# The opening of a fused attention and SoLU kernel: order of a table load, of loads, of masks and of a conversion

## The chip, the core and the metric

The kernel runs on one core of a Trainium2 chip. The time is the device time of one execution in microseconds (us); before the change it is 384.42 us, the median of four runs (383.80 to 385.46). The engines are named as in the profile: PE (TensorE matmuls; PEld its weight loads), DVE (VectorE), ACT (ScalarE), POOL (GpSimd), SP (SyncE, which here only issues DMAs).

## The reference

Gated linear attention over 4 batches x 8 heads, 768 tokens, head width 48, followed by a SoLU block with a normalisation on the same 3072 tokens (8 x 48 = 384 columns):

```python
for t in range(S):
    state = alpha[:, :, t, :, None] * state + einsum('bhd,bhe->bhde', k[:, :, t], v[:, :, t])
    y[:, :, t] = einsum('bhd,bhde->bhe', q[:, :, t], state)
...
h = x @ w_in                                  # 384 -> 1024
e = exp(h - max(h)); sm = e / (sum(e) + 1e-9)
solu = h * sm
ln = (solu - mean(solu)) / sqrt(var(solu) + 1e-6) * g_ln
out = ln @ w_out                              # 1024 -> 384
```

The inputs q, k, v and alpha are float32; the two weight matrices arrive as float64.

## The kernel before

The tokens are worked in G = 6 chunks of 128. In a chunk the recurrence is written as matrices: running products of alpha are applied to the keys and the queries, scores of 128 x 128 tokens are taken for each batch and head, masked to the lower triangle (by one mask, since the scores stand transposed), and multiplied with v; what earlier chunks contribute comes through a state. The four batches lie on four groups of 32 partitions. A head's first 32 columns fill such a group; the last 16 columns of two heads share one. So there are NB = 12 blocks: 8 of first columns and 4 of last columns, in three tiles of four blocks (tile 2 holds the last columns).

The whole order is written out by hand: each engine runs its instructions in the order of the program, and nothing reorders them. The change touches only the opening, that is the loads and chunk 0. There the steps are these, with their lines:

- DMA issues. SP issues alpha, k, q (two DMAs each, `load_first`, L153), v as one DMA of 768 KB into slot 0 of a buffer `room` (`load_v_first`, L188), then the first two weight requests (`fetch`, L559): three DMAs of 512 KB for the pieces 0 and 1 of w_in into slots 3 and 4, and three for the pieces 2 and 3 into slots 1 and 2. ScalarE issues four small ones (identity, mask, parity, gains; L640 to L644).
- POOL clears buffers (L647 to L653), then moves v from the slot into its padded place vn, the even and the odd heads apart (two copies, L190).
- PE warms up with 18 products of a constant tile (`warm`, L442; each call counts two records in the profile) and then turns alpha, k and q by products with the identity (`turned`, L171). ScalarE brings the last columns together first (`ends_of`, L162; its first instruction is preceded by the load of its function tables) and copies the turned alpha to SBUF (L671).
- DVE takes the running products (`scan_back` and `scan_on`, both L219), multiplies the turned keys (L679) and the turned queries (L689) by them: first tile 2 of the queries (`qe`), then tiles 0 and 1. ScalarE splits `qe` by parity (`apart`, L244) and checks alpha's range (`alpha_over`, L211).
- PE takes the scores (`scores`, L278) of the heads 0 to 3 into four PSUM banks, one for each batch, and of the heads 4 to 7 into four more. DVE multiplies all eight by the mask into `sT` (`masked`, L289).
- DVE converts piece 0 of w_in from float64 to float32 in five instructions (`bits`, L589, L592, L597, L600, L601). The function can also be called for its first two or its last three alone; so it is already used for later pieces.
- PE multiplies the masked scores with vn (`read_values`, L312): for each batch 16 products, all of a batch's heads; ScalarE copies the result out (L348). Then PE turns the gains (L612) and the keys back (`keys_back`, L297), and ScalarE copies those (L299) and checks the range of the pieces 0 and 1 (`in_range`, L576, L577), while DVE converts piece 1.
- After that the loop over f (from L708) runs the first up-projection (`up_mm`, L386), its exponentials (L400), products (L401) and squares (L402), between the conversions of the other pieces.

Later chunks overlap attention and the SoLU block in the same way. A second function, `general_path`, holds a slower version that runs only if the range checks fail; it is not run here.

Of the kernel before, what the change touches and what calls it, by code (L numbers as in the profile page):

```python
# [9 lines left out]
FP = mybir.dt.float32  # L10
# [4 lines left out]
ALU = mybir.AluOpType  # L15
AX = mybir.AxisListType
P = 128
# [15 lines left out]
def fast_path(ctx, tc, q, k, v, alpha, moe_w_in, moe_w_out, moe_g_ln, out):  # L33
# [12 lines left out]
    nc = tc.nc  # L46
    B, H, S, D = q.shape
# [4 lines left out]
    NP = H // 2  # L52
    NB = H + NP
# [8 lines left out]
    def pool(name, bufs, **kw):  # L62
        return ctx.enter_context(tc.tile_pool(name=name, bufs=bufs, **kw))
# [5 lines left out]
    small = pool("small", 4)  # L69
# [4 lines left out]
    ps_a = pool("ps_a", 1, space=PS)  # L74
# [4 lines left out]
    mask = const.tile([P, P], FP, name="mask")  # L79
# [7 lines left out]
    mhalf = const.tile([P, 1], FP, name="mhalf")  # L87
# [13 lines left out]
    qn = const.tile([P, H, TQ, D], FP, name="qn")  # L101
# [12 lines left out]
    all_of = [slice(0, D), slice(E1, VW)]  # L114
# [17 lines left out]
    sT = const.tile([P, B, H, P], FP, name="sT")  # L132
# [13 lines left out]
    def by_token(x):  # L146

        return x.rearrange("p h u d -> p (h u d)").rearrange("p (b h d) -> p b h d", b=B, h=H)
# [9 lines left out]
    def ends_of(src, tag=None):  # L158

        ends = ring.tile([P, T4], FP, name=tag) if tag else two.tile([P, T4], FP, tag="two", name="ends")  # L160
        ends = ends.rearrange("p (b d) -> p b d", b=B)
        nc.scalar.copy(out=ends.rearrange("p b (h d) -> p b h d", h=H), in_=by_token(src)[:, :, :, E0:D])  # L162
        return ends

    def turned(src, ends, out, blocks=range(NB)):

        x = by_token(src)
        for j in blocks:
            for b in range(B):
                cols = x[:, b, j, 0:E0] if j < H else ends[:, b, E0 * (j - H) : E0 * (j - H) + E0]  # L170
                nc.tensor.matmul(  # L171
                    out[j // NP][32 * b : 32 * b + 32, j % NP], lhsT=cols, rhs=ident, start=True, stop=True,
                    tile_position=(0, 32 * b), skip_group_check=True,
                )
# [8 lines left out]

    def load_v_first(slot):
        x = slots[slot].rearrange("p (n d) -> p n d", d=D)
        y = vn.rearrange("p b h d -> p (b h) d")
        xi, yi = (z.rearrange("p (n i) d -> p i n d", i=2) for z in (x, y))
        nc.sync.dma_start(out=x, in_=v[:, :, 0:P].rearrange("b h p d -> p (b h) d"))  # L188
        for i in range(2):
            nc.gpsimd.tensor_copy(out=yi[:, i, :, all_of[i]], in_=xi[:, i])  # L190


    def firsts(src, dst):
# [90 lines left out]
    masks = {}  # L284

    def masked(half, batches=range(B)):
        a = masks[half]
        for b in batches:
            nc.vector.tensor_tensor(  # L289
                out=sT[:, b, half * NP : half * NP + NP], in0=a[b], in1=mask[:, None, :].to_broadcast([P, NP, P]),  # L290
                op=ALU.mult,
            )
# [25 lines left out]
    def read_begin():  # L318
        reading["y"] = {}
        reading["begun"] = set()  # L320
# [19 lines left out]
    def read_values(g, batches=range(B)):  # L340
        if 0 in batches:
            gr[g]["x"] = pair.tile([P, KC, B, P], FP, name="x")
        for b in batches:
            for n, part in enumerate(parts):
                for a, r, h, e in part:
                    y_mm(b, a, r, 0, vn[:, b, h, e], sT[:, b, h], n == len(parts) - 1)
        for b in batches:
            nc.scalar.copy(out=gr[g]["x"][:, :, b], in_=reading["y"][b])  # L348
# [90 lines left out]
    def warm(n, ps=ps_o, tag="o"):  # L439
        t = ps.tile([P, 512], FP, tag=tag, name="warm")  # L440
        for i in range(n):
            nc.tensor.matmul(t[:, 0:P], lhsT=ones, rhs=ones, start=True, stop=True)  # L442
# [99 lines left out]
    def place(i):  # L542
        kind, f = pieces[i]
        return w_out[:, f : f + 2, 0:DM] if kind else w_in[:, :, f * P : f * P + 2 * P]
# [3 lines left out]
    def fetch(i, slot, n=1):  # L548

        kind, f = pieces[i]  # L550
        w = n * F // (2 if kind else KC)
        raw = room[:, 1536 * slot : 1536 * (slot + n)].bitcast(U32).rearrange("p (c f w) -> p c f w", f=w, w=2)
        if kind:
            parts = [(slice(0, P), c, moe_w_out[(f + c) * P : (f + c + 1) * P, :]) for c in range(2)]
        else:
            parts = [(slice(0, P), c, moe_w_in[c * P : (c + 1) * P, f * P : f * P + w]) for c in range(KC)]
        for rows, c, src in parts:
            if float64:
                nc.sync.dma_start(out=raw[rows, c].rearrange("p f w -> p (f w)"), in_=src.bitcast(U32))  # L559
            else:  # L560
                dst = w_out[rows, f + c, 0:DM] if kind else w_in[rows, c, f * P : f * P + w]
                nc.sync.dma_start(out=dst, in_=src)
        for m in range(n):
            raws[i + m] = raw[:, :, w // n * m : w // n * (m + 1)]
# [14 lines left out]
    def bits(i, part=None):  # L579
        if not float64:  # L580
            return
        lo, hi = raws[i][:, :, :, 0], raws[i][:, :, :, 1]
        if part != 1:
            made[i] = [
                two.tile([P, F], FP, tag="two", name=x).rearrange("p (c f) -> p c f", c=hi.shape[1])
                for x in ("top", "low")
            ]
            top = made[i][0].bitcast(U32)
            nc.vector.tensor_scalar(  # L589
                out=top, in0=hi, scalar1=3, scalar2=0x3FFFFFF8, op0=ALU.logical_shift_left, op1=ALU.bitwise_and  # L590
            )
            nc.vector.scalar_tensor_tensor(  # L592
                out=top, in0=hi, scalar=0xC0000000, in1=top, op0=ALU.bitwise_and, op1=ALU.bitwise_or
            )
        if part != 0:
            top, low = made.pop(i)
            nc.vector.tensor_scalar(  # L597
                out=low.bitcast(U32), in0=top.bitcast(U32), scalar1=0xFF800000, scalar2=None, op0=ALU.bitwise_and
            )
            nc.vector.scalar_tensor_tensor(out=low, in0=lo, scalar=2.0**-52, in1=low, op0=ALU.mult, op1=ALU.mult)  # L600
            nc.vector.tensor_tensor(out=place(i), in0=low, in1=top, op=ALU.add)  # L601
# [49 lines left out]
    nc.gpsimd.memset(hT[:, NB * SW : NB * SW + 2], 1.0)  # L651
    nc.gpsimd.memset(seed, 0.0)
    nc.gpsimd.memset(state, 0.0)  # L653
    load_v_first(0)
    fetch(0, 3, 2)
    fetch(2, 1, 2)
    nc.vector.memset(ones, 1.0)
    nc.vector.memset(small_ones, 1.0 / 32)
# [4 lines left out]
    def three(name, where):  # L663
        return [pool.tile([P, NP, P], FP, tag=tag, name=f"{name}{i}") for i, (pool, tag) in enumerate(where)]


    warm(18)
    t = three("tp_a", [(ps_a, "a0"), (ps_a, "a1"), (ps_a, "a2")])
    turned(an, ends_of(an), t)
    for i in range(3):  # L670
# [2 lines left out]
    t = three("tp_k", [(ps_a, "a3"), (ps_h, "h"), (ps_h, "h")])  # L673
# [5 lines left out]
        nc.vector.tensor_tensor(out=kT[:, part], in0=t[i], in1=hk[:, part], op=ALU.mult)  # L679
    scan_on(0, 0)  # L680
    t = three("tp_q", [(ps_o, "o"), (ps_o, "o"), (ps_a, "a0")])
    turned(qn, ends_of(qn), t)

    warm(2, ps_a, "a1")
    for i in (2, 0, 1):
        if i == 1:
            scan_on(0, i)
# [2 lines left out]
            out=qe if i == 2 else qv[:, part], in0=t[i], in1=aT[:, part, 1:SW], op=ALU.mult  # L690
# [4 lines left out]
    t = [x.tile([P, NP, P], FP, tag=n, name="a_" + n) for x, n in ((ps_h, "h"), (ps_o, "o")) for _ in range(2)]  # L695
    scores(0, 1, t)
    read_begin()
    masked(0)
    masked(1)
    bits(0)  # L700
    read_values(0)
    gains()
    keys_back(0)
# [4 lines left out]
    for f in range(FC):  # L708
        p = 2 + f // 2
# [215 lines left out]
    def compare(out, x, bound, op):  # L925
# [6 lines left out]
        out=chunks[:, :, 2], in0=sums[:, :, 2], scalar=0.25, in1=sums[:, :, 3], op0=ALU.mult, op1=ALU.is_le  # L932
# [6 lines left out]
    else:  # L939
# [9 lines left out]
        out=bad, in0=all_ok[0:1, 0:1], scalar1=float(P * ends[-1]), scalar2=None, op0=ALU.is_lt  # L949
# [415 lines left out]
def kernel(tc, *args):  # L1365

    with ExitStack() as ctx:
        taken = fast_path(ctx, tc, *args)
    with tc.If(taken > 0):
        general_path(tc, *args)  # L1370
# [30 lines left out]
```

## Time and profile before

| What | Value |
|---|---|
| median of four runs | 384.42 us |
| the profiled execution | 385.19 us |
| its span in the profile | 383.4 us |
| granted TensorE clock | 0.998 |
| PE busy (matmuls) | 367.8 us, 96% of the span |
| DVE, ACT, POOL busy | 245.2, 144.4 and 126.0 us |
| HBM read and written | 25.30 and 4.72 MB |

The span is what the engines did; the execution's time is 1.8 us longer. The page cuts the span into 40 slices of 9.6 us and shows how busy each engine was in each, in tenths (9 is 90% or more):

```profile
PE   8879999879899999999999999999999999999995
DVE  0988888996989866893565884665885411444410
ACT  2618775284526244124252224351224131233110
POOL 5020000041045990544521553630562520333210
DMA  9982989303447200961000960001500000000011
```

The opening is the first three digits: PE waits now and then (8, 8, 7), DVE starts in the second slice, and the DMA engines are full until some 27 us. A busy PE is not PE at its peak: its matmuls are pipelined and their ends are modelled.

### The profile page before, as it was taken

What the parts mean: (1) busy time and instruction counts of PE and PEld (TensorE: products, weight loads), DVE (VectorE), ACT (ScalarE), POOL (GpSimd) and SP (SyncE); (2) the same over time, 40 slices, a digit from 0 to 9 for tenths busy, and PEclk for the clock granted to TensorE, in tenths of its full rate; (3) what the DMA queues carried; (4) which work ended last, traced back from release to release, by engine and by line L of the source; (5) the groups of instructions that cost most, each with busy time, mean ns of one, the idle gap of its engine ahead of it and who ended that gap; (6) DMA issues with size and microseconds to landing.
All of it is one profiled execution on the core that took longest, in us unless ns stands there. A gap on an engine that the chain in (4) does not pass through costs nothing.

```text
span 383.4 us, 10525 instructions
## 1 busy us (share of the span) xinstructions
PE 367.8 (96%) x4665; PEld 222.1 (58%) x4665; DVE 245.2 (64%) x381; ACT 144.4 (38%) x258; POOL 126.0 (33%) x132
## 2 busy tenths in 40 slices
PE   8879999879899999999999999999999999999995
PEld 8776345547655656555666555575555665555552
DVE  0988888996989866893565884665885411444410
ACT  2618775284526244124252224351224131233110
POOL 5020000041045990544521553630562520333210
PEclk9999999999999999999999999999999999999999
DMA  9982989303447200961000960001500000000011
GB/s 184 197 297 71 231 261 181 85 21 91 117 111 121 43 4 4 174 151 47 22 3 24 199 148 24 23 10 31 89 0 22 22 24 2 21 21 21 22 45 47
DMA packets 65510, 30.78 MB, mean 80 GB/s; under 512 B 47016, under 2 KB 63664, under 8 KB 65456
## 3 DMA queue, kind: packets, MB, share of 16 engines
q1 hardware_dynamic: 64432, 29.10, 34.2%
q8 instruction: 38, 0.62, 0.7%
q10 hardware_dynamic: 1024, 0.92, 0.7%
q14 instruction: 16, 0.13, 0.1%
HBM read 25.30 MB, written 4.72 MB: 78 GB/s over the span
## 4 chain that ended last, share of the span: by engine, by line
PE 70%; DVE 18%; ACT 6%; issue 3%; DMA 1%; SPq 0%; POOL 0%; DVEq 0%; ACTq 0%
PE o L497 28%; PE h L386 23%; PE y L312 8%; PE a L278 5%; DVE aT L219 3%; DVE hT L219 3%; DVE room L401 2%; PE warm L442 2%; DVE sT L289 1%; ACT sq L576 1%; DVE aT L194 1%; DMA an<-in_alpha_dram 1%; PE kv L361 1%; DVE top L592 1%; ACT sq L577 1%
## 5 line engine op out<-in xcount | busy, mean ns | idle before, releaser
L497 PE MATMUL o<-w_out,room 128*128 128x385 f32 x384 | 133.6, 491 | 2.4 <-DVE o_mean L523 2.4
L386 PE MATMUL h<-x,w_in 128*128 128x512 f32 x288 | 132.1, 598 | 0.4 <-DVE room L401 0.4
L497 PEld LDWEIGHTS o<-w_out,room 128*128 128x128 f32 x384 | 71.3, 190 | 58.5 <-issue 15.9
L386 PEld LDWEIGHTS h<-x,w_in 128*128 128x128 f32 x288 | 53.0, 189 | 59.0 <-issue 48.4
L401 DVE TENSOR_TENSOR room<-h,e 128x512 f32<-128x512 f32 x40 | 27.6, 689 | 82.9 <-ACT e L400 82.7
L400 ACT ACTIVATE e<-h 128x512 f32<-128x512 f32 x40 | 23.9, 597 | 108.6 <-PE h L386 108.6
L527 POOL TENSOR_TENSOR r<-sums,mhalf 128x1 f32<-128x1 f32 x20 | 14.3, 714 | 138.7 <-DVE sums L519 138.7
L417 POOL TENSOR_TENSOR p<-p,e 128x512 f32<-128x512 f32 x30 | 41.8, 1393 | 15.7 <-ACT e L400 15.7
L402 ACT ACTIVATE u<-room 128x512 f32<-128x512 f32 x40 | 25.2, 630 | 35.1 <-DVE room L401 35.1
L289 DVE TENSOR_TENSOR sT<-a,mask 128x512 f32<-128x512 f32 x44 | 27.3, 681 | 9.8 <-PE a L278 9.6
L219 DVE TENSOR_TENSOR_SCAN hT<-aT,unit 128x516 f32<-128x516 f32 x18 | 23.2, 1357 | 8.7 <-ACT aT L671 8.7
L240 POOL TENSOR_TENSOR kT<-kT,hT 128x1024 f32<-128x1024 f32 (+1 forms) x8 | 14.2, 1794 | 43.6 <-DVE kT L194 34.7
L278 PEld LDWEIGHTS a<-qv,kT 32*128 32x128 f32 x704 | 22.3, 186 | 9.2 <-issue 3.5
L278 PE MATMUL a<-qv,kT 32*128 32x128 f32 x704 | 25.5, 279 | 2.0 <-DVE qv L689 0.8
L219 DVE TENSOR_TENSOR_SCAN aT<-aT,seed 128x516 f32<-128x516 f32 x18 | 27.1, 1539 | 0.2
L417 DVE TENSOR_TENSOR p<-p,u 128x512 f32<-128x512 f32 x30 | 23.0, 766 | 6.5 <-ACT u L402 6.5
L312 PE MATMUL y<-sT,vn 128*32 128x128 f32 x768 | 24.0, 274 | 3.0 <-issue 2.1
L312 PEld LDWEIGHTS y<-sT,vn 128*32 128x32 f32 x768 | 21.2, 110 | 5.3 <-issue 3.9
L211 ACT ACTIVATE sq<-an,mone 128x1536 uint8<-128x1536 f32 x12 | 18.9, 1571 | 0.2
L312 PE MATMUL y<-qv,state 32*32 32x128 f32 x960 | 16.8, 277 | 0.1
L529 ACT ACTIVATE o_sb<-o,r 128x384 f32<-128x384 f32 x16 | 9.3, 580 | 18.7 <-POOL r L527 18.7
L312 PEld LDWEIGHTS y<-qv,state 32*32 32x32 f32 x960 | 12.1, 103 | 7.3 <-issue 5.2
(140 smaller groups left out, 368.3 us busy)
## 6 DMA issues: line engine op xcount, KB each, us to landing
an<-in_alpha_dram SPq DMA_DIRECT2D x20, 192.0 KB, 4.0
vn<-in_v_dram SPq DMA_DIRECT2D x10, 384.0 KB, 5.4
out_dram<-o_sb SPq DMA_DIRECT2D x20, 192.0 KB, 1.9
room<-in_moe_w_in_dram SPq DMA_DIRECT2D x6, 512.0 KB, 8.4
room<-in_moe_w_out_dram SPq DMA_DIRECT2D x8, 384.0 KB, 4.0
kn<-in_k_dram SPq DMA_DIRECT2D x16, 192.0 KB, 4.3
qn<-in_q_dram SPq DMA_DIRECT2D x16, 192.0 KB, 3.6
kn<-in_k_dram SPq DMA_DIRECT2D x4, 384.0 KB, 5.7
```

What stands on the lines that cost most here:

```text
L211: nc.scalar.activation(out=sq, in_=x, func=AF.Relu, scale=sign, bias=mone, accum_out=over[:, g, i : i + 1])
L219: nc.vector.tensor_tensor_scan(out=o, data0=a, data1=s, initial=1.0, op0=ALU.mult, op1=ALU.add)
L278: nc.tensor.matmul(a[b][:, i], lhsT=kT[quarter(b), kb], rhs=qv[quarter(b), qb], start=kb == h, stop=kb != h, tile_position=(32 * b, 0), sk ...
L289: nc.vector.tensor_tensor(out=sT[:, b, half * NP : half * NP + NP], in0=a[b], in1=mask[:, None, :].to_broadcast([P, NP, P]), op=ALU.mult,)
L312: nc.tensor.matmul(y_bank(b)[quarter(r), a], lhsT=lhsT, rhs=rhs, start=(b, r) not in begun, stop=stop, tile_position=(row, 32 * r), skip_g ...
L386: nc.tensor.matmul(h, lhsT=w_in[:, a, f * P : (f + 1) * P], rhs=d["x"][:, a].rearrange("p b t -> p (b t)"), start=(a == 0), stop=(a == KC ...
L400: nc.scalar.activation(out=e, in_=h, func=AF.Exp)
L401: nc.vector.tensor_tensor(out=u, in0=h, in1=e, op=ALU.mult)
L402: nc.scalar.activation(out=u2, in_=u, func=AF.Square)
L417: eng.tensor_tensor(out=p, in0=d[0][i] if f == 1 else p, in1=d[f][i], op=ALU.add)
L497: nc.tensor.matmul(d["o"][:, 0 : DM + 1], lhsT=u_of(g, f)[:, b * P : b * P + P], rhs=w_out[:, f], start=(f == 0), stop=(f == FC - 1), skip ...
L527: nc.gpsimd.tensor_tensor(out=r, in0=s[:, 3:4], in1=mhalf, op=ALU.pow)
```

## The change

Seven things are done in the opening; nothing of what is computed changes.

1. The DMA of v is issued after the three DMAs of the weight pieces 0 and 1, and before those of 2 and 3.
2. Moving v to its place becomes a function of its own, `place_v`. It runs on ScalarE, and later in the program: after the scores.
3. ScalarE copies one column of a constant ahead of the opening's work, so that its table load stands in front of that copy, right behind its four DMA issues, and no longer in front of the first copy of alpha.
4. The warm-up in front of alpha has 16 products instead of 18, the one ahead of the scores 1 instead of 2.
5. The turned queries are made in the order tile 0, tile 2, tile 1.
6. The first two instructions of the conversion of piece 0 come ahead of the masks, the last three behind them.
7. The masks of the heads 0 to 3 for the batches 2 and 3 leave DVE: ScalarE copies these two score tiles to `sT`, and GpSimd multiplies them there by the mask. DVE keeps the other six.

```diff
     def load_v_first(slot):
         x = slots[slot].rearrange("p (n d) -> p n d", d=D)
+        nc.sync.dma_start(out=x, in_=v[:, :, 0:P].rearrange("b h p d -> p (b h) d"))
+        return x
+
+    def place_v(x):
         y = vn.rearrange("p b h d -> p (b h) d")
         xi, yi = (z.rearrange("p (n i) d -> p i n d", i=2) for z in (x, y))
-        nc.sync.dma_start(out=x, in_=v[:, :, 0:P].rearrange("b h p d -> p (b h) d"))
         for i in range(2):
-            nc.gpsimd.tensor_copy(out=yi[:, i, :, all_of[i]], in_=xi[:, i])
+            nc.scalar.copy(out=yi[:, i, :, all_of[i]], in_=xi[:, i])
...
-    load_v_first(0)
     fetch(0, 3, 2)
+    v_first = load_v_first(0)
     fetch(2, 1, 2)
...
-    warm(18)
+    nc.scalar.copy(out=small.tile([P, 1], FP, name="t"), in_=mhalf)
+    warm(16)
...
-    turned(qn, ends_of(qn), t)
-    warm(2, ps_a, "a1")
+    turned(qn, ends_of(qn), t, [*range(NP), *range(H, NB), *range(NP, H)])
+    warm(1, ps_a, "a1")
...
     read_begin()
-    masked(0)
+    bits(0, 0)
+    for b in (2, 3):
+        s = sT[:, b, 0:NP]
+        nc.scalar.copy(out=s, in_=masks[0][b])
+        nc.gpsimd.tensor_tensor(out=s, in0=s, in1=mask[:, None, :].to_broadcast([P, NP, P]), op=ALU.mult)
+    place_v(v_first)
+    masked(0, range(2))
     masked(1)
-    bits(0)
+    bits(0, 1)
     read_values(0)
```

## The prediction

> **What bounds the kernel now.** I read the page first: PE is busy 96% of the span, so whatever comes out of the opening comes out of the end, unless a wait takes it back. Then the chain that ended last, in order of time (start, length, what), for the stretch that is edited:
>
> ```profile
> 1.05 6.91 PE warm L442 x36
> 7.96 1.05 PE tp_a L171 x32
> ...
> 9.73 3.49 DVE hT L219 x3
> ...
> 21.88 3.07 DVE sT L289 x5
> 24.95 0.04 issue
> 24.99 0.85 PE y L312 x17
> 25.84 0.78 issue
> 26.62 3.25 PE y L312 x105
> ```
>
> The reader sees: PE's warm-up until 7.96, alpha turned, a DVE stretch from 9.73 to 20.84 with hardly a gap, the masks (21.86 to 26.73), PE's y (24.99 to 29.87). After it come the turned keys and, from 30.64, ScalarE with kg and the range checks. So the number to follow is where y ends.
>
> Then the timeline of single engines (start, length, engine, line, shapes, idle before):
>
> ```profile
> 6.76 1.28 ACT L162 ACT_TABLE_LOAD   x1 [6.76 <-DMA an<-in_alpha_dram]
> 8.05 0.62 ACT L162 COPY ends<-an 128x512 f32<-128x512 f32 x1
> ```
> ```profile
> 18.90 1.84 POOL L190 COPY vn<-room 128x768 f32<-128x768 f32 x1 [13.44 <-DMA room<-in_v_dram]
> ```
> ```profile
> 9.96 3.06 SPq L188 DMA_DIRECT2D room<-in_v_dram  x1
> ```
> ```profile
> 36.54 2.82 SPq L153 DMA_DIRECT2D kn<-in_k_dram  x1
> ```
>
> and what SP's queue had moved (packets, MB) by 13.03, 14, 18, 26 and 38.3 us:
>
> ```profile
> q1 hardware_dynamic: 12235, 2.33, 99.7%
> ```
> ```profile
> q1 hardware_dynamic: 12450, 2.37, 94.3%
> ```
> ```profile
> q1 hardware_dynamic: 16497, 3.22, 103.1%
> ```
> ```profile
> q1 hardware_dynamic: 17265, 5.98, 101.7%
> ```
> ```profile
> q1 hardware_dynamic: 17588, 6.94, 76.2%
> ```
>
> Alpha, k and q are 2.36 MB. When SP was done issuing v (13.03), 2.33 were gone; at 14 hardly any of v had followed. So v was issued only as its predecessors left, and began to flow about 1.0 us after: the queue stood idle for it. V then took from 14.05 to 17.95 (3.9) and landed at 18.86, 0.95 later.
>
> **The change, part by part.**
>
> *Warm-up.* 30 of the 36 records run from 1.05 to 7.12 (0.20 each), the last six at 0.14. Two calls (four records) less are worth 0.56 at the fast rate, 0.81 at the slow one; I take 0.6. It counts because alpha's second half is there at 6.7 (issued at 1.22, 5.5 to landing), before the new end at 7.36.
>
> *Table load.* 1.28 us move from behind alpha to behind ScalarE's four DMA issues, which end at 2.78: 2.8 to 4.1. The added one-column copy waits for a memset that ends at 1.03 and costs some 0.2 (as fend's), hidden by the wait for alpha that is queued behind it. Unmoved, the load and the ends copy would hold ScalarE to 8.67, while the first turned alpha would be there at 8.4: 0.2 saved, part of the 0.6 and not more.
>
> *Order of q's blocks, one warm call less.* The third tile of q is turned a third (32 records, 1.0) earlier. DVE wants it at 17.69 now and 17.1 then; PE finished it at 17.64. q's second half lands at 14.8 whatever is done here, so without the new order 0.5 of the 0.6 would be lost; with it the tile is ready at 16.7. The second tile is ready at 17.6 and wanted at 19.55: nothing. The warm call lies in PE's wait for the queries: nothing.
>
> *DVE.* It is free at 20.84, now 20.24. The half conversion (0.94 + 0.96 and gaps, 1.93) fills what was a wait for the scores (1.01) and ends at 22.17; two masks at 0.62, then four: the first one that y waits for ends at 24.03 (was 24.88), the last at 25.9 (was 26.73). The other half conversion (0.56 + 0.96 + 0.96 and gaps, 2.56) ends at 28.45 instead of 31.16. That has slack: the first up-projection also waits for the turned keys (31.48). The half needs the first three weight DMAs by 20.24; see below, 18.6.
>
> *Two masks elsewhere.* ScalarE copies two score tiles at about 21.25 (0.59 and 0.52, to 22.35), where it idled 7.5 us. GpSimd's two products: 1.19 (L251) to 1.39 (L417, mean) each, so 23.6 and 24.9. They are wanted for the third and fourth batch of y, which start 2.6 and 3.5 us after y. Late here would cost one for one. The bound on the other side is the vn copy on GpSimd: 1.84 while DVE ran a scan, 0.82 for its twin: add 1.0 to each and they end at 24.2 and 26.6, still in time for a y from 24.1. Here a rule speaks against the change: the Trainium skill (SBUF — State Buffer, SBUF: two separate sides) says that DVE and GpSimd share a port pair held exclusively for a whole instruction, so that the loser waits. By it DVE's second conversion step (two SBUF inputs) holds off the first product until 22.15, and nothing is lost on y; the row with 1.84 agrees with the direction.
>
> *v into place on ScalarE.* GpSimd's 2.61 go; ScalarE's two copies cost 0.84 (L577, the same 768 columns) and about 0.76, with the wake-up 1.7 in all after v has landed, not before 22.35. What is queued behind: the four x copies, which wait for y anyway. So y's release, T, is the later of 24.1 and v's landing plus 1.7. Before, v's wait cost nothing (in place at 21.5, wanted at 23.7).
>
> *The loads.* No bytes more, but SP's queue now brings three weight DMAs (1.57 MB) before v. From 18 to 26 the weights ran at 2.76 MB in 8 us, 0.345 per us: 4.55 us. They are issued at 0.43 each while q still flows, so they follow q at 13.1 and are gone at 17.65, landed at 18.6. For v's start I have three rows. Lower bound: v is issued while the weights flow and follows at once: landed at 17.65 + 3.9 + 0.95 = 22.5. Second: like v now, issued when its predecessors have left, flowing 1.0 later: 23.5. Upper: kn's second half at 36.54 sat behind two w_out DMAs (end at 7.08 MB, so about 38.65) and its issue ended only at 39.36, 0.7 later still: 24.2. The nearest row is v itself, a request of 768 KB; I take 23.5.
>
> *Sum.* y's first waits. Before: release 24.99, end 29.87. In it is a stall of 0.78 that follows no wait: the trace shows such stalls of PE that end at 14.03 (0.72), 20.43 (0.36) and 26.62, the last two 127 matmul records apart. With six records less ahead of it, it stays in y's first batch. The release sits four records further into y, so the end is T + 4.78. With v at 23.5: T = 25.2, end 30.0, 0.1 after before. At the lower bound: T = 24.2, end 29.0, 0.9 earlier. At the upper: T = 25.9, end 30.7, 0.8 later. Everything after (turned keys, kg, ScalarE's checks and exponentials to about 60 us) hangs on that end and shifts with it; DVE's 2.7 us are not passed on: its next stage waits for ScalarE's exponential (36.73, after 0.98 of idling), and kg on ScalarE waits for PE's turned keys, not for DVE.
>
> On instruction blocks the Trainium skill (Runtime: NRT & Kernel Launch, Instruction fetch mechanics) says that streams are refilled in blocks of 256 instructions and the crossing is mostly hidden. 128 matmul records with their weight loads would be such a block, but the rows show up to 0.78 open. By the page y would be 0.78 shorter in both kernels, so the difference stays; by the rows it is lost in both.
>
> The profiled run took 385.19: the span of 383.4 and 1.8 around it, 0.77 above the median of 384.42. It would become 385.3; on the median, 384.5.
>
> **The rivals.**
>
> *v in time* (383.2). v's issue overlaps the weights and the release is DVE's 24.1. For it: the weights are few, large packets, and four of their requests were issued at 0.43 each with half of v still under way. Against it: the empty microsecond before v. Gain 0.9; with 0.8 instead of 0.6 from the warm-up or part of the 0.78 stall covered by the longer wait in front of y, as at 20.43 (0.36), up to 1.7; centre 1.2.
>
> *v later still* (385.7). The upper bound, and the same empty microsecond ahead of the weights, whose first issue took 3.34 us behind v: then they start at 14.1 and all is 1.0 later: landed at 25.2, T = 26.9, end 31.7, 1.8 after before. From 0.8 to 1.8, centre 1.3. It decides when v lands after 23.4, where T + 4.78 passes 29.87; from 24.5 it is beyond 0.3%. For it: the kn row. Against it: q's backlog at 9.96 covers small requests.
>
> **How the numbers follow.** Forecast (v about a microsecond late, the gains eaten): 0.38. v in time: 0.35, 0.29 of it beyond 0.3% (1.15 us, about what a measurement of this kernel can tell from no change). v later still: 0.27, nearly all of it beyond, as nothing else is at hand to win it back. Rounded: faster 0.30, same 0.43, slower 0.27. The forecast's own range is 384.0 to 385.2 (v at 23.0 to 24.2); with the others until two in ten are left: 383.0 to 385.7.
>
> **What would show it.** Right: a second copy of vn on ScalarE that ends just before y starts, idle ScalarE before it put down to v's DMA, v landing near 23.5, about a microsecond of empty queue after the weights; y's end within 0.5 of 29.9; the first w_in piece converted by 28.5, well before its use. Wrong: v landing before 22.5, or y waiting for DVE; a GpSimd product that y waits for; the half conversion waiting for weights after 20.24; a PE stall moved out of y.

## The result and the profile after

The changed kernel takes 386.33 us, the median of 52 runs (383.90 to 388.23); the kernel before, beside it, 384.67 us (78 runs, 383.46 to 389.64). The ratio is 1.0031, 95% interval [1.0019, 1.0044]: slower by 0.3%, so by about as much as can be told; the two medians alone lie 1.66 us apart. Single executions that took far longer than the others of their kernel are left out of medians and ratios. The profiled execution took 386.95 us, its span 385.2 us (before 383.4), at a mean granted clock of 0.991 (before 0.998).

The chain that ended last, of the changed kernel, in order of time (start, length, what), from v's request to the end of y:

```profile
15.29 9.44 DMA room<-in_v_dram
24.81 1.57 ACT vn L193 x2
26.43 5.07 PE y L315 x120
31.50 0.15 PE tp_g L615
```

v has taken the place that DVE's masks had in this chain before. It landed at 24.73, ScalarE placed it by 26.38, and y ended at 31.50 instead of 29.87. That is 1.63 us later, and the first up-projection starts 1.63 us later too (32.95 for 31.32).

The opening ahead of it did gain. The timeline of DVE and POOL in the changed kernel (start, length, engine, line, shapes, idle before and its releaser) shows the first running product at 8.93 (9.73 before), and then where a part of the gain was lent out:

```profile
8.93 3.48 DVE L222 TENSOR_TENSOR_SCAN hT<-aT,unit 128x516 f32<-128x516 f32 x3 [7.87 <-ACT aT L676]
...
21.25 1.93 DVE L595 SCALAR_TENSOR_TENSOR top<-room,top 128x768 uint32<-128x768 uint32 x1
```
```profile
21.10 3.21 POOL L707 TENSOR_TENSOR sT<-sT,mask 128x512 f32<-128x512 f32 x2 [15.64 <-ACT sT L706]
```

The second conversion step took 1.93 us instead of 0.96 while GpSimd multiplied two tiles by the mask beside it (its first product had begun 0.15 us ahead of that step), so DVE's masks began at 23.10, not 22.17. The last of GpSimd's products was there at 24.31. Nobody waited for either: y waited for v.

SP's requests in the timeline of the changed kernel, and what its queue had moved (packets, MB) by 14, 18.5 and 23 us:

```profile
10.08 3.18 SPq L562 DMA_DIRECT2D room<-in_moe_w_in_dram  x1
...
15.29 0.43 SPq L186 DMA_DIRECT2D room<-in_v_dram  x1
```
```profile
q1 hardware_dynamic: 12348, 2.37, 96.0%
...
q1 hardware_dynamic: 12767, 3.80, 95.8%
...
q1 hardware_dynamic: 16848, 4.78, 101.7%
```

Alpha, k and q are 2.36 MB. At 14 us hardly anything of the weights had moved: the request that now stands seventh, the first of the weights, took 3.18 us to issue, and the queue stood nearly empty behind it. By the single packets of the trace, the weights' 1.57 MB started between 13.90 and 19.52 us, and v's 4096 packets of 192 bytes between 18.53 and 24.18. The 16848 packets at 23 us are not all of v: the next weights began at 22.43 beside it. From 23 us to v's landing the queue still moved

```profile
DMA packets 211, 0.43 MB, mean 250 GB/s; under 512 B 110, under 2 KB 110, under 8 KB 211
```

and 96 of the 110 small ones are v's (the other 14 have 4 bytes).

PE in the changed kernel, and then the same stretch cut into microseconds (stretch, its length, busy time and count of PE, PEld, DVE, ACT and POOL, granted clock, DMA share, GB/s):

```profile
25.69 0.43 PE L315 MATMUL y<-sT,vn 128*32 128x128 f32 x8 [3.52 <-ACT vn L193]
26.43 5.07 PE L315 MATMUL y<-sT,vn 128*32 128x128 f32 x120 [0.31 <-ACT vn L193]
```
```profile
25.00:26.00 1.00, 0.31 (x8) 0.16 (x8) 1.00 (x2) 1.00 (x2) 0.00 (x0) 1.00 0.84 320
26.00:27.00 1.00, 0.69 (x18) 0.54 (x16) 1.00 (x3) 0.37 (x1) 0.00 (x0) 0.67 0.99 352
27.00:28.00 1.00, 1.00 (x28) 0.89 (x24) 0.97 (x2) 0.00 (x0) 0.00 (x0) 0.50 0.74 287
28.00:29.00 1.00, 1.00 (x26) 0.89 (x22) 0.97 (x2) 0.48 (x1) 0.00 (x0) 0.50 0.18 74
29.00:30.00 1.00, 1.00 (x28) 0.93 (x24) 0.22 (x1) 0.29 (x1) 0.00 (x0) 0.63 0.00 0
```

The reader sees the wait of 3.52 us in front of y, and a granted clock that falls to half just when y begins: 1.00, 0.67, 0.50, 0.50, 0.63. In a microsecond at 0.50 some 27 products pass. The lost clock adds up to 0.33 + 0.50 + 0.50 + 0.37 = 1.70 us. In the windows of the kernel before, PE stays at 1.00 through this stretch, for example

```profile
27.00:28.00 1.00, 1.00 (x47) 1.00 (x41) 0.97 (x2) 0.48 (x1) 0.00 (x0) 1.00 0.24 86
```

### The profile page after: what moved, and what is told of

Same layout as the page of the kernel before. It is cut to its first block, busy times and chain, and to the rows that moved or that the text cites. A ratio compares the mean times of both kernels' runs of the same rounds, so it can differ in the third digit from the quotient of the medians.

```text
span 385.2 us, 10520 instructions
## 1 busy us (share of the span) xinstructions
PE 369.1 (96%) x4659; PEld 222.4 (58%) x4659; DVE 244.9 (64%) x379; ACT 147.2 (38%) x263; POOL 126.6 (33%) x132
## 4 chain that ended last, share of the span: by engine, by line
PE 71%; DVE 13%; SPq 5%; DMA 5%; ACT 3%; issue 2%; POOL 0%; DVEq 0%; ACTq 0%
PE o L500 29%; PE h L389 25%; PE y L315 9%; PE a L281 4%; SPq L153 3%; DMA room<-in_v_dram 2%; DMA an<-in_alpha_dram 2%; DVE aT L222 2%; DVE hT L222 2%; PE kv L364 1%; DVE room L404 1%; SPq L562 1%; DVE aT L197 1%; PE tp L300 1%; SPq L141 1%
## 5 line engine op out<-in xcount | busy, mean ns | idle before, releaser
L500 PE MATMUL o<-w_out,room 128*128 128x385 f32 x384 | 135.3, 496 | 2.4 <-DVE o_mean L526 2.4
L500 PEld LDWEIGHTS o<-w_out,room 128*128 128x128 f32 x384 | 72.1, 192 | 59.3 <-issue 17.8
L292 DVE TENSOR_TENSOR sT<-a,mask 128x512 f32<-128x512 f32 x42 | 26.1, 681 | 9.5 <-PE a L281 9.5
L315 PE MATMUL y<-sT,vn 128*32 128x128 f32 x768 | 25.2, 285 | 4.3 <-ACT vn L193 3.8
L315 PEld LDWEIGHTS y<-sT,vn 128*32 128x32 f32 x768 | 22.2, 115 | 6.9 <-ACT vn L193 4.3
L281 PE MATMUL a<-qv,kT 32*128 32x128 f32 x704 | 24.5, 278 | 0.7 <-ACT qv L247 0.3
```

The costliest lines, as they stand in the source:

```text
L281: nc.tensor.matmul(a[b][:, i], lhsT=kT[quarter(b), kb], rhs=qv[quarter(b), qb], start=kb == h, stop=kb != h, tile_position=(32 * b, 0), sk ...
L292: nc.vector.tensor_tensor(out=sT[:, b, half * NP : half * NP + NP], in0=a[b], in1=mask[:, None, :].to_broadcast([P, NP, P]), op=ALU.mult,)
L315: nc.tensor.matmul(y_bank(b)[quarter(r), a], lhsT=lhsT, rhs=rhs, start=(b, r) not in begun, stop=stop, tile_position=(row, 32 * r), skip_g ...
L500: nc.tensor.matmul(d["o"][:, 0 : DM + 1], lhsT=u_of(g, f)[:, b * P : b * P + P], rhs=w_out[:, f], start=(f == 0), stop=(f == FC - 1), skip ...
```

## The experiments

All times are medians; a ratio is that to the kernel before, run beside it on the same chip, with its 95% interval. The kernels before had medians from 384.12 to 385.11 us in these comparisons. "Record" is one matmul record in the profile; a product of float32 makes two.

### Keep PE busy during the wait

The changed kernel, with 12 products of a constant tile on PE after the scores:

```diff
     place_v(v_first)
+    warm(12, ps_a, "a3")
     masked(0, range(2))
```

> The changed kernel, and PE runs 12 more products of the constant tile (24 records, 3.4 us at 0.14) between the scores and y, in the wait for v. Theory (v late, and PE's idle stretch of 3.5 us then costs granted clock: 0.50 from about 26.3 to 29.6 in the changed kernel's profile): y's release stays at 26.4, the clock stays 1.00 through y, y ends near 30.2 instead of 31.5, and the time falls by 1.0 to 1.5 us against the changed kernel. Rival (the lateness of v alone, 26.43 against 24.99, makes the loss): y and the time stay as they were, within 0.3 us.

384.58 us (384.18 to 388.85), ratio 1.0018 [0.9992, 1.0044]. In its PE timeline, and in its windows:

```profile
26.30 3.48 PE L315 MATMUL y<-sT,vn 128*32 128x128 f32 x120 [0.31 <-ACT vn L193]
...
82.77 4.52 PE L500 MATMUL o<-w_out,room 128*128 128x385 f32 x8 [2.39 <-DVE o_mean L526]
```
```profile
27.00:28.00 1.00, 1.00 (x48) 1.00 (x41) 0.72 (x1) 0.48 (x1) 0.00 (x0) 1.00 0.05 20
```

y starts as late as in the changed kernel (26.30 for 26.43), yet its 120 records take 3.48 us instead of 5.07, at a clock of 1.00 and 48 records to the microsecond. So the fall of the clock, and not v's lateness by itself, makes y end at 31.50; with PE kept busy it ends at 29.78, before the kernel before (29.87). The trace shows this outright, for y. In the medians it is the difference between 1.66 us above the kernel before and 0.46 us above it, by the ratios between 1.2 and 0.7; the intervals of the two ratios overlap. The second line, an output product of 4.52 us where the kernel before has 2.83, is a second place where the clock falls; it is taken up below.

The changed kernel's own 54 executions (the profiled ones among them) say the same by their mean granted clock: seven at 0.996 or more took 383.90 to 385.17 us (median 384.84), seventeen at 0.992 to 0.995 had a median of 386.12, and thirty below that one of 386.83. The kernel before loses clock too: beside the experiments, 34 of its 104 executions lay below 0.992, with a median of 386.7 us; the other 70 had one of 384.1. And with the clock whole the changed kernel still lies 0.7 us above it (384.84 in seven executions, 384.12 in 51 at 0.996 or more): a good half of the loss goes with the clock, the rest does not.

### The loads and the conversion as before

The changed kernel, but v's request ahead of all weights again, and the conversion of piece 0 whole and behind the masks:

```diff
-    fetch(0, 3, 2)
     v_first = load_v_first(0)
+    fetch(0, 3, 2)
...
-    bits(0, 0)
...
-    bits(0, 1)
+    bits(0)
```

> The changed kernel with v's DMA ahead of the weights again and the whole conversion of piece 0 behind the masks, as before; table load, warm-up, order of q's blocks, the two masks on ScalarE and GpSimd and v's placing on ScalarE stay. Theory (v's place in the queue is what costs): v lands near 18.9, y is released by DVE's mask at about 23.1 to 23.6 (no PE idle over 2 us), y ends near 27.9 to 28.4, 1.5 to 2 us ahead of before; the conversion ends at about 29.4 and the first up-projection starts just behind the turned keys at 29.6; time 1.2 to 2 us under before. Rival (moving masks and v to ScalarE and GpSimd costs by itself, through the port they share with DVE): no faster than before.

382.73 us (382.39 to 384.17), ratio 0.9958 [0.9934, 0.9982]: faster than both. ScalarE placed v from 21.79 on, and y waited for DVE's mask and then stood once, without a wait that shows:

```profile
23.34 1.07 PE L315 MATMUL y<-sT,vn 128*32 128x128 f32 x23 [0.23 <-DVE sT L292]
25.29 3.04 PE L315 MATMUL y<-sT,vn 128*32 128x128 f32 x101 [0.88 <-issue]
```

y ended at 28.33. So parts 1 and 6 of the change cost what the others gain, and more. The rival, that the moved work costs by itself, falls: this kernel has all of it. (It speaks of a port that ScalarE, too, shares with DVE; no run here shows one.)

### The order of the loads alone

The kernel before, with only v's request moved behind the three weight requests:

```diff
-    load_v_first(0)
     fetch(0, 3, 2)
+    load_v_first(0)
     fetch(2, 1, 2)
```

> The kernel before with one edit: the three DMAs of weight pieces 0 and 1 ahead of v. Theory: v lands at 24.7, GpSimd has it in place at about 26.4, y is released there instead of at 24.99, after PE has idled 2.3 to 2.7 us; time 1.0 to 1.5 us over before if the clock holds, 2 to 3 over if it falls. Rival (the order of the loads is harmless, as GpSimd had v at 21.5 and y wanted it at 24): within 0.3 us of before.

385.19 us (383.47 to 386.57), ratio 1.0025 [1.0007, 1.0044]. v landed at 24.04 here, GpSimd placed it:

```profile
25.74 3.48 PE L312 MATMUL y<-sT,vn 128*32 128x128 f32 x120 [0.20 <-POOL aT L203]
...
31.45 2.81 PE L386 MATMUL h<-x,w_in 128*128 128x512 f32 x6 [0.61 <-DVE g_col L613]
```

PE idled only 1.02 us before y, since the scores end later without the gains of the opening, and the clock stayed at 1.00. y ended at 29.22, earlier than before, for the stall of 0.78 us that y has before was spent inside the wait. Then the up-projection waited 0.61 us for DVE. The late v is nearly free in this profile; it is the same lateness behind an earlier opening that makes the long wait. But the median lies 1.07 us above that of the kernel before, about what the theory had for a clock that holds. The clock is not the reason: the five executions at 0.996 or more have a median of 384.99, the 19 such of the kernel before, beside them, one of 384.12. This one profile, whose y ends 0.65 us ahead, does not show where that time goes; it stays open.

### The table load, the warm-up and the order of q's blocks alone

The kernel before with parts 3, 4 and 5:

```diff
-    warm(18)
+    nc.scalar.copy(out=small.tile([P, 1], FP, name="t"), in_=mhalf)
+    warm(16)
...
-    turned(qn, ends_of(qn), t)
-    warm(2, ps_a, "a1")
+    turned(qn, ends_of(qn), t, [*range(NP), *range(H, NB), *range(NP, H)])
+    warm(1, ps_a, "a1")
```

> The kernel before with the table load ahead of alpha, 16 and 1 warm-up products, and the new order of q's blocks; nothing else. Theory: everything from the first turned alpha to y is 0.6 to 0.8 us earlier (DVE's scan at 8.93 as in the changed kernel, y ending near 29.1), time 0.5 to 0.8 us under before. Rival (the shorter warm-up leaves PE's clock lower later, or the gain is eaten behind y): no difference.

383.14 us (382.36 to 386.48), ratio 0.9984 [0.9962, 1.0006]. The running products start 1.0 us earlier (8.73 for 9.73), and y gains more than that:

```profile
23.28 1.07 PE L312 MATMUL y<-sT,vn 128*32 128x128 f32 x23 [0.98 <-DVE sT L289]
24.96 3.04 PE L312 MATMUL y<-sT,vn 128*32 128x128 f32 x101 [0.62 <-issue]
```

y ended at 28.00, 1.87 us earlier. Most of the rest is in the scores of the heads 0 to 3: they take 2.11 us in this chain, and 2.76 in that of the kernel before, with a stall of 0.36 in them. This is the change's gain: 1.0 us in the medians, 0.6 by the ratio, whose interval just includes no change. The kernel with v ahead, above, has two masks moved off DVE and v placed by ScalarE besides and is at 382.73: these moves add nothing that the intervals can tell.

### v ahead, half a conversion ahead of the masks

The changed kernel with v's request first, the half conversion left where the change puts it:

```diff
-    fetch(0, 3, 2)
     v_first = load_v_first(0)
+    fetch(0, 3, 2)
```

> The changed kernel with one edit: v's DMA ahead of the weights again; the half conversion stays ahead of the masks. Theory (the order of the loads is there for the half conversion, the two belong together): the weights land at about 23 to 25, DVE waits for them at 20.1 with six masks queued behind, y is released only at 26 to 28 and PE idles 4 us or more; time at or above that of the changed kernel, 1 to 3 us over before. Rival (the half conversion is harmless, v's place alone made the loss): within 0.5 us of e2_v_first, 1.4 us under before.

389.19 us (388.38 to 389.94), ratio 1.0109 [1.0075, 1.0142].

```profile
24.85 0.95 DVE L592 TENSOR_SCALAR top<-room 128x768 uint32<-128x768 uint32 x1 [5.09 <-DMA room<-in_moe_w_in_dram]
```
```profile
27.55 0.64 PE L315 MATMUL y<-sT,vn 128*32 128x128 f32 x4 [5.66 <-DVE sT L292]
```

DVE waits 5.09 us for the weights with all its masks queued behind, PE idles 5.66 us, and the clock is at 0.50 from 25 to 31 us. So the order of the loads and the half conversion belong together: the half conversion ahead of the masks needs the weights first, the masks' consumer needs v first, and the queue carries one after the other.

### PE kept busy at 82 us

The clock also fell at the first output product of chunk 0, which follows 2.4 us of idling, in the profiles of the changed kernel and of two others of the seven that leave this wait unfilled, and not in that of before:

```profile
84.47 4.46 PE L500 MATMUL o<-w_out,room 128*128 128x385 f32 x8 [2.38 <-DVE o_mean L526]
```

Seven products were put ahead of it, in three kernels: that with the table load and warm-up alone, that with v ahead, and the kernel before.

```diff
+    warm(7, ps_a, "a2")
     down(2, 0)
```

> e4_table_warm (before with table load, warm-up and order of q's blocks) and PE running 7 products of the constant tile in its idle stretch of 2.4 us at about 80 to 82 us. Theory (an idle stretch there costs granted clock in some executions, as in the changed kernel's profile, where the same eight o matmuls took 4.46 us at a clock of 0.57 and 2.83 at 1.00 before): the executions above 384.4 become rare, the median falls to about 382.8. Rival (those executions have another cause, or the added products delay o): median at e4's 383.1 or above.

> e2_v_first with the same 7 products at 80 to 82 us. Theory: its profile lost clock there (0.73 and 0.85 in two stretches of 4 us), so it falls from 382.7 to about 381.5; the best of all. Rival: unchanged at 382.7.

> The kernel before with the same 7 products at 80 to 82 us. Theory: its executions above 385.5 (5 of 30 in the last comparison) become rare and the median falls by 0.2 to 0.5 us. Rival: no difference.

383.32 us, ratio 0.9957 [0.9929, 0.9984] (383.14 and 0.9984 without); 383.16 us, 0.9946 [0.9919, 0.9973] (382.73 and 0.9958 without); 384.46 us, 0.9986 [0.9961, 1.0012] for the kernel before. All three held a clock of 0.996 or more in every execution, and none gained what these intervals can tell; the second had been expected 1.2 us lower. So the fall at 82 us is real but is not where the time goes.

The profile of the third lost clock in y, with nothing of the opening changed:

```profile
26.30 4.91 PE L312 MATMUL y<-sT,vn 128*32 128x128 f32 x107 [1.22 <-issue]
```
```profile
27.00:28.00 1.00, 1.00 (x28) 0.96 (x24) 0.97 (x2) 0.48 (x1) 0.00 (x0) 0.50 0.15 49
```

The same 107 records took 3.25 us in the profile of before. PE had idled 0.91 and 1.22 us here, with 17 records between them. This execution took 386.00 us, the only other one of this kernel below 0.997 took 386.60, and the ten above had a median of 384.33. So a fall of the clock in y goes with some 2 us of the whole time also where v is in time.

The second was run again:

> The same kernel as e7_v_first_busy82, beside e9 on one chip: 382.3 to 383.3, ratio to before 0.993 to 0.998.

382.71 us (381.96 to 387.54), ratio 0.9948 [0.9913, 0.9983]. It is the best version found: by the ratios 2.0 us below the kernel before and 3.2 below the changed one. Whether its seven products do anything is not shown.

### PE kept busy at both places

The changed kernel with both fills, run twice:

```diff
     place_v(v_first)
+    warm(12, ps_a, "a3")
     masked(0, range(2))
...
+    warm(7, ps_a, "a2")
     down(2, 0)
```

> The changed kernel with both fillings: 12 products in the wait for v and 7 at about 80 to 82 us. Theory (the loss of the changed kernel is v's lateness, which without the loss of clock leaves it level with before, plus about 1.7 us for each stretch at half clock): clock at 0.996 or above in nearly all executions, y ending at 29.7 as in e1_busy_pe, 0.2 ahead of before's 29.87; median 383.5 to 384.2, level with before without its slow-clock executions and 0.5 to 1.2 us behind e7_v_first_busy82. Rival (something else in the change costs too): 385 or more.

385.92 us (385.00 to 389.76), ratio 1.0019 [0.9987, 1.0052]. That is over a microsecond more than the theory had, at a clock of 0.996 or more in eleven of twelve executions; the rival, that something else in the change costs too, had 385 or more. In its trace the clock is whole, y ends at 29.97 and the output product at 82.84 starts level with before (82.89); at 96.6 both are still level. Then PE stands twice inside the next two batches of y. The same kernel once more:

> The kernel with both fills and 38 added records once more, beside the one with 128 added. Theory 'added records move the block ends': 385.3 to 386.2 again, and its profile shows two stalls of 0.8 to 1.1 us between 98 and 104 us. Theory 'the time of that run was chance': 383.5 to 384.5 in this one, level with the one with 128 added.

385.77 us (384.97 to 386.59), ratio 1.0023 [0.9997, 1.0049]: not chance. The PE timeline of the kernel before, and of this second run:

```profile
100.20 1.95 PE L312 MATMUL y<-sT,vn 128*32 128x128 f32 x63
103.11 2.02 PE L312 MATMUL y<-sT,vn 128*32 128x128 f32 x65 [0.95 <-issue]
```
```profile
98.88 1.18 PE L315 MATMUL y<-qv,state 32*32 32x128 f32 x64 [0.55 <-issue]
...
100.45 1.08 PE L315 MATMUL y<-sT,vn 128*32 128x128 f32 x32
102.89 2.83 PE L315 MATMUL y<-sT,vn 128*32 128x128 f32 x96 [1.36 <-issue]
```

Before, PE stands 0.95 us after the 63rd record of this batch; here 0.55 and, 128 records later, 1.36 after the 32nd. Between the output products at 82.61 and 105.64 this kernel loses 0.87 us on the one before (82.89 and 105.05), and the stalls sum to 1.91 against 0.95. Where they sit can be counted. The changed kernel has 6 records less ahead of this point (three products fewer), the fills add 24 and 14: 32 more than before, and 63 - 32 = 31. With the first fill alone it is 18 more, and its stall sits after record 45 = 63 - 18; with the second alone 8 more, and record 55 = 63 - 8. PE stands at every 128th record, so a product added anywhere moves all later stalls. Counted from the first record of a trace, the stalls that show in the scores, in y and in the fill stand behind the records 350, 477, 605, 1371, 1498 and 1627, within one, in whichever kernel.

So that these ends fall back where the changed kernel has them, the fill in the wait was then made of 114 small records, 128 with the other 14:

```diff
-    warm(12, ps_a, "a3")
+    fill(57)
...
+    def fill(n):
+        t = ps_a.tile([P, 512], FP, tag="a3", name="warm")
+        for i in range(n):
+            r = quarter(i % 4)
+            nc.tensor.matmul(t[r, 0:96], lhsT=ones[:, 0:32], rhs=ones[:, 0:96], start=True, stop=True,
+                tile_position=(0, r.start), skip_group_check=True)
```

> The changed kernel with products on TensorE in both empty stretches, as in the run with both fills, but in a number that adds 128 records of TensorE in all (57 small products in the wait for v, 114 records; 7 ahead of the output product at 82 us, 14 records) where that run added 38. What is behind: in the run with both fills the clock was whole and y ended level with the kernel before, yet the runs lay at 385.9; its profile shows 0.82 us of 'issue' inside y at 99.39 and 1.08 at 103.12, where the kernel before has 0.95 at 103.11 alone, and 0.46 at 201.50 where it has 0.42 at 143.70. Theory 'TensorE stands at block ends, and added records move them': with 128 added every block ends at the product where it ends in the changed kernel, which has only 0.30 us of visible issue after 30 us; the time falls to 383.8 to 384.8, 1.0 to 1.8 us below the run with 38 added, at a clock of 0.996 or more. Theory 'the fills themselves cost it, or the later start of y': 385.5 to 386.3 as before. A third: the 114 records hold a block's end of their own that comes after 25.7 us and delays y by up to 1 us; then y ends at 30.5 or later and the time is 384.8 to 385.5.

387.50 us, ratio 1.0071 [1.0038, 1.0104]. The third theory held in its mechanism; its 385.5 us were passed by 2:

```profile
24.85 1.93 PE L451 MATMUL warm<-ones 128*32 128x96 f32 x83 [1.15 <-issue]
...
30.71 4.02 PE L315 MATMUL y<-sT,vn 128*32 128x128 f32 x87 [2.66 <-issue]
...
105.04 2.17 PE L315 MATMUL y<-sT,vn 128*32 128x128 f32 x70
107.98 1.93 PE L315 MATMUL y<-sT,vn 128*32 128x128 f32 x58 [0.77 <-issue]
```

The small products brought a stall of their own (1.15), and the next came 2.66 us long in the middle of y, with the clock down to 0.50 behind it; y ended at 34.73. Where the stalls sit came out as counted: after record 70 for 63 + 6 = 69. As a test of what the moved stalls cost in time it decides nothing, since its own new stall outweighs them. So it is shown where the profile of the kernel with both fills loses 0.87 us, and that the places move with the records; that this time comes back when the places do was not shown.

## Why the prediction was wrong, step by step

The forecast was 384.5 us with a range of 383.0 to 385.7; the changed kernel takes 386.33. Its y should have ended at 30.0 and ended at 31.50: y's release came 1.2 us later than in the sum, and y took 0.3 us longer from there.

- *Warm-up, table load, q's order*: right. The running products start 0.80 us earlier (taken 0.6, bounds 0.56 to 0.81), the table load is at 2.81 for 1.28 us, and the scores of both tiles end with PE going idle at 22.2. Alone these parts give 1.0 us in the medians, 0.6 by the ratio.
- *DVE and the two masks elsewhere*: the size of one term was off. The half conversion was to end at 22.17 and ended at 23.18. The Trainium skill (SBUF — State Buffer, SBUF: two separate sides) has the one of DVE and GpSimd that starts first hold their common ports for its whole instruction and the other wait, and the prediction took DVE's step for the first. Here GpSimd's first product was (21.10, for 1.27 us), and DVE's step of 0.96, begun at 21.25, took 1.93. In the kernel with the first fill it was the other way round:

```profile
20.72 0.96 DVE L595 SCALAR_TENSOR_TENSOR top<-room,top 128x768 uint32<-128x768 uint32 x1
```
```profile
20.88 1.93 POOL L707 TENSOR_TENSOR sT<-sT,mask 128x512 f32<-128x512 f32 x1 [15.42 <-ACT sT L706]
```

So the rows agree with the page, and the order taken was wrong. It cost nothing, because v was later still.
- *v into place on ScalarE*: right, 1.65 us from landing to the end of the copies (taken 1.7).
- *The loads*: this step failed, and its mis-sized term is v's own passage. The prediction said of the weights that "they follow q at 13.1 and are gone at 17.65, landed at 18.6", had v flow from 1.0 us behind them, so from 18.65, and land 3.9 + 0.95 = 4.85 us after that, at 23.5, with 24.2 for an upper bound. Measured: the first weight request took 3.18 us to issue, the weights ran from 13.90 to 19.52, and v's first packet came at 18.53, among their last ones. So v's start came out by luck: the empty microsecond stood ahead of the weights, as the rival "v later still" had it, and none stood ahead of v. From its first packet to its landing v then took 6.20 us: 24.73, which is 1.2 us over the value taken and 0.5 over the bound. In the six profiles with v behind the weights this passage took 5.81 to 6.40 us, and v landed at 24.02 to 24.79. In the eight with v first it took 4.99 to 5.90, and the one row that the forecast had, that of the kernel before, is the shortest of them. The empty microsecond does not decide: with the first fill 2.49 MB had moved by 14 us, so the weights followed q at once, and v still landed at 24.60. Why v passes more slowly there was not tried; in the changed kernel its packets share the queue with the last of these weights until 19.52 and with the next ones from 22.43.
- *y's length, "the end is T + 4.78"*: this step failed in two terms of opposite sign. The stall of 0.78 was kept in y; behind the long wait none shows, and with the clock whole y ends 3.53 us after its release (26.25 to 29.78 in the chain of the kernel with the first fill). So at a clock of 1.00, T = 26.38 would have given 29.9: just what was forecast, by luck, since y's length was too long by as much as v was too late. But the prediction has no term for PE's clock. The wait that it foresaw in front of y, longer for an earlier end of the scores, brings the clock to half, which adds 1.6 us (5.12 against 3.53). That is the missing term, and what puts y's end beyond the forecast's. With the clock whole the changed kernel's median is 384.84, inside the range; the 0.7 us by which this lies above the kernel before is not explained.
- *The rivals*: "v in time" fell: v landed 2.2 us after its 22.5. "v later still" had the mechanism of v and, with 385.7 and an end of y at 31.7, nearly the number. But its T was 0.5 too late and its y had a stall that was not there in place of the clock that was. The row that speaks for the first of them was misread: three weight requests, not four, were issued in about 0.43 us each while v was under way, from 16.45 us on; the fourth took 1.58.
- *What is not passed on*: right in the direction. What y loses stays lost: the up-projection starts 1.63 us later, the span is 1.8 longer.

The Trainium skill (TensorE: Matmul & The Clock Gate, What's actually happening) states that TensorE's clock is halved after an idle window of about 3.4 us and comes back after as long a busy one, in windows that run freely. The row here, 3.52 us of idling with 3.4 us at about half clock behind it, agrees; by that rule a step of its own would have been due in the prediction as soon as it forecast a wait of about 3 us in front of y. The falls after 2.4 us of idling at 82 us, and after 0.91 and 1.22 us in the kernel before with its fill there, came after less.

## What to carry to other kernels

When a change lets PE finish earlier but not its next operand arrive earlier, the longer wait can cost more than itself: add up PE's idle time in front of dense work, and where it comes to some 2 us or more, reckon with a stretch at half clock in some executions. What such a fall costs depends on its place: in y some 2 us of the whole time went with it, at 82 us nothing that could be told. When two requests on one queue change places, the price of each is not carried over with it: the slow issue and the empty stretch stayed near their place in the queue, and v took longer to pass behind the weights than ahead of them (5.81 to 6.40 us against 4.99 to 5.90). A product added to a stream of short ones moves every later stall of PE, so a fill is judged by the whole trace, not by the wait that it fills.

## What the runs showed of the hardware

- PE stands at every 128th matmul record where the records are short: 0.20 to 1.36 us in y where it shows, and 2.66 us where the 128 records ahead had passed in 3.2 us after another stall. Among the long products of the up-projection no such stall shows. The Trainium skill (Runtime: NRT & Kernel Launch, Instruction fetch mechanics) calls the crossing of a block of 256 instructions mostly hidden; 128 records with their weight loads are 256, and in these rows it is not hidden.
- The granted clock fell to 0.50, for 3.4 us, after 3.52 us of idling. It fell after only 2.4 us in three of seven profiles (ahead of the first output product of chunk 0), and after 0.91 and 1.22 us with 17 records between them in one; not after 1.02 us, nor after 0.84 and 0.78 us in the kernel before. In the wait of 5.66 us (v ahead, half a conversion ahead of the masks) it fell before the wait was over and stayed down twice as long.
- A DVE step that reads two tiles of SBUF and a GpSimd product did not run beside each other: the one that began second took longer by most of what the other still had to run (1.93 for 0.96 us on DVE, 1.93 for 1.27 on GpSimd). DVE's masks, which read one tile of SBUF and one of PSUM, held nothing up (0.68 and 1.28 us beside each other in the kernel with v ahead).
- The seventh request on SP took about 3 us to issue in eight of the fourteen profiles, whichever it was (v 3.06 before, the first weights 3.18 after and 2.94 with the loads alone); in the other six it was the sixth (2.70 to 3.11). Kernels with the same opening showed both. Why is open; it was not tried apart.
- v landed 0.42 to 0.68 us after the end of its last packet in all fourteen profiles, wherever its request stood.
